# A ninth chunk of an attention and MoE kernel by seven block products, with a new order of work

## The chip, the core and the metric

The kernel runs on one core of a Trainium2 chip. The metric is the device time of one execution in microseconds (us). Engines are called as in the profile: PE (TensorE), DVE (VectorE), ACT (ScalarE), POOL (GpSimd), SP (SyncE, which issues the DMAs).

## What is computed

Attention with a block-causal mask on 8 images of 576 tokens and 8 heads of 64, then a feed-forward layer with a squared ReLU on all 4608 tokens of width 512:

```python
scores = np.where(mask, (q @ k.T) / 8, -1e9)     # block i sees blocks j <= i, 64 tokens each
attn = exp(scores - max) / (sum + 1e-9)
x = (attn @ v)                                   # 4608 x 512
out = np.maximum(x @ w_in, 0) ** 2 @ w_out       # 512 -> 2048 -> 512
```

Inputs are float32. The kernel writes each float32 operand of the feed-forward layer as a sum of two float16 parts, high and low, and multiplies high by high, high by low and low by high: three float16 matmuls for one.

## The kernel before

**Work and its names.** A *pass* is one pair of heads of one image (40 in all, from A0 to A39). A is its scores on PE, B the row maxima on DVE, C the exponentials on ACT, S and R the sums and their inverse, H and L the high and low float16 part of the probabilities (L, the remainder, on DVE), T their transposes by DMA, G the product with the values on PE, X its copy out of PSUM into the tokens `x`. For a part of an image, sq, sa and nq square the tokens (ACT), add them (DVE) and sum them over partitions (PE); hb and xm scale them, ia and ib carry the scale to the output. Passes come in pieces (`A25_0`, `A25_1`, `A25_2`).

The feed-forward layer works on *chunks* of 384 tokens, 12 in all, in the order 0, 1, 2, 4, 3, 5, 7, 6, 8, 10, 9, 11 (`turn_of`, L973). The hidden layer of a chunk has 16 pieces of 128.

- **Plain chunks** (`plain`, L975; the first PLAIN = 4 in order: 0, 1, 2 and 4). Each piece f is a unit (`unit`, L1124): ph, 12 matmuls of 384 columns on PE; pos, the ReLU out of PSUM on ACT; sqr, the square on ACT; top, the high float16 part of the hidden layer (DVE or ACT); rem, its remainder (DVE or POOL).
- **The other eight** are multiplied in 2 x 2 blocks by seven products instead of eight (`group_steps`, L1231). A group is four pieces; a chunk has four groups. A product (p1, p2, p6, p5, p7, p4, p3, in that order) is two times six matmuls of 192 columns. They share two PSUM banks: X takes p1, p6, p7, p4 and is copied out after each (c11, c12, c22, c21), B takes p2, p5, p3 and is added to such a copy after each (a11, a22, a12, DVE). So p6 waits for c11, p7 for c12, p5 for a11, p4 for c22, p3 for a22. Then come sq (ReLU and square), top and rem for each block. These products need combinations of the tokens (s1 to s4, of which h.. and l.. are the parts) and of the weights: the *turned weights* (`turn_steps`, L1182), 18 steps per group, t0_0 to t3_17, each an addition or subtraction of a 128x512 tile, a cast or a remainder. Steps 0 to 12 fill `turned_w`; steps 13 to 17 overwrite a part of w1 and so come after the last plain chunk.

The output of a chunk (`out_steps`, L1348) is three blocks po_0 to po_2 of 16 steps of three matmuls of 512 columns; ob scales a block out of PSUM, out stores it. `out_ring` (L1169) gives the outputs of the first PLAIN - 1 chunks the two banks `pair0` and `pair1`, later ones `pair0` alone. At the first product of a group `bank_of` (L416) closes `pair1` and `side1` and puts three banks `group0` to `group2` there.

**The order.** `plan_all` (L1410) names every task with its queue, what it follows, and which buffers it takes and frees. At run time none of this is read: `Plan.run` (L383) goes through the list ORDER (L104), which was searched beforehand, pops each task and calls it, with the engine that stands behind a colon (D, A, P):

```python
for word in ORDER.split():
    name, _, way = word.partition(":")
    make = self.tasks.pop(name)[3]
    if way: make(WAYS[way])
    else:   make()
```

Each engine works through its instructions in that order; semaphores hold an instruction until its operands are there. All instructions are recorded through `Queue.call` (L328), so the profile shows line 329 for all of them: they are told apart by their tiles.

## Time and profile before

| | us |
|---|---|
| median of 3 runs (lowest, highest) | 976.61 (975.47, 978.28) |
| profiled execution | 977.2 |
| its span, first to last instruction | 975.4 |
| PE busy in it | 941.6 |
| DVE busy | 795.4 |
| ACT busy | 599.8 |
| POOL busy | 264.5 |

An engine's busy time counts each moment in which one of its instructions runs. Matmuls are pipelined and their ends are modelled, so a matmul's own duration (246 ns for 192 columns) is longer than its distance to the next; the chain of waits gives that distance, as the length of a piece over its number of matmuls. `_AluOpType.subtract` is the tile of the turned weights in the making, `r` the hidden layer's float32 tile, `hidden` its float16 parts, `pair` the bank of plain units and outputs, `group` those of the seven products, `side` that of the scores, `px` that of the product with the values.

### The profile page before, as it was taken

Reading aid. Unit: us, or ns where it says so; the run is one execution under the profiler, and the core shown is the slowest. Engines: PE = TensorE matmul, PEld = TensorE weight load, DVE = VectorE, ACT = ScalarE, POOL = GpSimd, SP = SyncE. Lnnn points to the kernel's source line nnn. Section 1 sums busy time; section 2 is a strip of 40 time slices with the busy share of each in tenths; the row PEclk is TensorE's granted clock in tenths of the full one; section 3 lists DMA queues with packets and bytes.
Section 4 is the critical chain, followed back from the end, with each engine's and each line's share of the span. In section 5 each row is a group of like instructions: output and inputs, shape, how many; then the busy total and the mean of one; then the engine's idle time right before and its main releaser. Section 6 shows DMA issues by size and latency. Waiting matters only on the chain.

```text
span 975.4 us, 20874 instructions
## 1 busy us (share of the span) xinstructions
PE 941.6 (97%) x8001; PEld 593.2 (61%) x8001; DVE 795.4 (82%) x1769; ACT 599.8 (61%) x1510; POOL 264.5 (27%) x366
## 2 busy tenths in 40 slices
...
GB/s 360 326 123 168 163 134 101 165 174 174 83 128 117 122 100 121 111 74 121 148 96 140 41 163 79 153 118 100 91 161 119 90 99 90 79 13 1 23 2 44
DMA packets 221649, 114.92 MB, mean 118 GB/s; under 512 B 195290, under 2 KB 203756, under 8 KB 221548
## 3 DMA queue, kind: packets, MB, share of 16 engines
...
## 4 chain that ended last, share of the span: by engine, by line
PE 72%; DVE 18%; DMA 4%; issue 3%; ACT 2%; POOL 1%; SPq 1%; DVEq 0%; POOLq 0%; ACTq 0%
PE pair L329 37%; PE group L329 21%; PE side L329 7%; DVE p_rows L329 5%; PE px L329 5%; DVE nmx L329 3%; DVE w L329 2%; PE po L329 2%; DMA first<-in_qk 2%; DVE r L329 2%; DVE hidden L329 1%; DMA hidden<-in_w_in 1%; ACT p L329 1%; DVE xt_all L329 1%; DVE x L329 1%
## 5 line engine op out<-in xcount | busy, mean ns | idle before, releaser
L329 PE MATMUL pair<-w,hidden 128*128 128x512 f16 (+1 forms) x1680 | 382.1, 377 | 1.6 <-DVE ob L329 1.6
L329 PEld LDWEIGHTS <-hidden 128*128 128x128 f16 x1776 | 169.5, 98 | 179.7 <-issue 11.8
L329 PEld LDWEIGHTS <-w 128*128 128x128 f16 x2304 | 201.4, 98 | 74.3 <-issue 16.3
L329 ACT ACTIVATE p<-side,nmx 128x256 f32<-128x256 f32 (+8 forms) x264 | 139.7, 538 | 111.7 <-DVE nmx L329 80.5
L329 POOL TENSOR_TENSOR hidden<-r,hidden 128x384 f16<-128x384 f32 x101 | 104.0, 1040 | 228.5 <-ACT hidden L329 216.0
L329 DVE SCALAR_TENSOR_TENSOR p_rows<-p,rs,p_rows 128x128 f16<-128x128 f32 (+6 forms) x264 | 147.5, 581 | 9.8 <-ACT p_rows L329 6.7
L329 PE MATMUL group<-xt_all,w 128*128 128x192 f16 x1536 | 142.9, 246 | 1.6 <-DVE r L329 1.4
L329 DVE TENSOR_REDUCE nmx<-side 128x1 f32<-128x192 f32 (+8 forms) x288 | 123.3, 479 | 18.5 <-PE side L329 18.0
L329 PE MATMUL pair<-xt_all,w 128*128 128x384 f16 x768 | 131.1, 326 | 2.0 <-ACT r L329 1.2
L329 POOL TENSOR_SCALAR sm<-sm 128x2 f32<-128x2 f32 (+2 forms) x104 | 34.3, 330 | 351.6 <-ACT p L329 337.2
L329 ACT ACTIVATE r<-r 128x384 f32<-128x384 f32 x208 | 106.8, 522 | 33.0 <-DVE r L329 30.5
L329 PE MATMUL group<-xt_all,turned_w 128*128 128x192 f16 x1152 | 108.9, 246 | 0.3 <-DVE r L329 0.3
L329 PEld LDWEIGHTS <-turned_w 128*128 128x128 f16 x1152 | 96.1, 98 | 12.2 <-issue 3.5
L329 PE MATMUL side<-qk 64*64 64x512 f32 (+2 forms) x480 | 97.2, 500 | 3.4 <-ACT p L329 1.9
L329 PE MATMUL side<-ks,qk 64*64 64x128 f32 (+4 forms) x576 | 92.3, 425 | 0.1
L329 ACT CAST hidden<-r 128x384 f16<-128x384 f32 x156 | 76.5, 508 | 19.3 <-DVE r L329 17.0
L329 DVE SCALAR_TENSOR_TENSOR r<-group,rescale,r 128x384 f32<-128x384 f32 x96 | 58.3, 612 | 33.7 <-PE group L329 26.8
L329 ACT ACTIVATE r<-group,rescale 128x384 f32<-128x384 f32 x72 | 41.4, 577 | 59.5 <-PE group L329 51.7
L329 ACT ACTIVATE p_rows<-p,rs 128x64 f16<-128x64 f32 (+9 forms) x124 | 61.9, 525 | 19.3 <-DVE rs L329 15.1
L329 DVE TENSOR_SCALAR p_rows<-p,rs 128x384 f16<-128x384 f32 (+9 forms) x156 | 68.6, 456 | 1.8 <-DMA p_turned<-p_rows 0.5
L329 PE MATMUL px<-p_turned,v 128*64 128x384 f16 (+5 forms) x1168 | 67.2, 269 | 1.7 <-ACT wt L329 1.4
L329 PEld LDWEIGHTS <-v 128*64 128x64 f16 x1128 | 49.1, 110 | 21.1 <-issue 8.8
...
## 6 DMA issues: line engine op xcount, KB each, us to landing
...
```

Source lines behind the costliest of these rows:

```text
L329: i = make(*a, **k)
```

## The change

PLAIN goes from 4 to 3, so chunk 4, the fourth in order, is computed by seven products too: nine of twelve chunks. It needs the turned weights, so all 72 steps now stand ahead of or within chunk 4's groups, and the last five of each group follow chunk 2, not chunk 4. The output of chunk 2 moves from two banks to one. ORDER is a new list of 4048 tasks (4012 before), with other engines for many of them. The lists of what a task follows and frees gain entries.

```diff
-PLAIN = 4
+PLAIN = 3
 ORDER = """
-p0 A0 B0 C0 S0 A1 r0 B1 C1 p1 prelu0_0 r1 A2 r2 prelu0_1 bits0_0 max0_0 S1 R0 prelu0_2 D0:D R1 D1:P p2 r3 B2 C2 bits0_1 A3 bits0_2 S2 bits0_3 B3 C3 E0
+p0 A0 B0 C0 p1 A1 r0 A2 S0 B1 C1 S1 R0 D0:D B2 R1 max0_0 prelu0_0 bits0_0 C2 r1 prelu0_1 A3 p2 bits0_1 E0 B3 C3 join0_0 r2 join0_1 prelu0_2 S2 r3 A4
...
-                over = {x: [f"po{prev}_2_{4 * g + int(x[1]) + 1}"] for x in ("11", "12", "21", "22")}
+                over = {x: [f"po{prev}_{m}_{4 * g + int(x[1]) + e}" for m in ((0, 1), (1, 2))[int(x[0]) - 1] for e in (-1, 1)] for x in ("11", "12", "21", "22")}
...
-                    ends = [(opener, z) for z in ("xt0", "xt1")] if g == NQ - 1 else []
+                    ends = [(opener, z) for z in ("xt0", "xt1")]
...
-                over = [f"po{prev}_2_{f}"] if ck else []
+                over = [f"po{prev}_{m}_{f}" for m in range(3)] if ck else []
...
-            add(f"X{i}_1", {"ACT": 440, "DVE": 490}, 0, [f"G{i}_1"], base + YR[3], lambda q, t=t: values_out(t, 1, q), frees=[(f"G{i}_1", "x")])
+            add(f"X{i}_1", {"ACT": 440, "DVE": 490}, 0, [f"G{i}_1", "l1_0" if t["b"] == 0 else "l0_1"], base + YR[3], lambda q, t=t: values_out(t, 1, q), frees=[(f"G{i}_1", "x")])
...
-                        if hp == 0:
-                            pb = b - 1 if g else (b - 1 if b > NT else 0)
-                            past = ([f"l{pb}_{g}"] if plain(chunk_of(pb, g)) else [f"l23{pb}_{g}", f"l6{pb}_{g}"]) if pb >= 0 else []
-                        else:
-                            past = []
+                        pb = b - 1 if g else (b - 1 if b > NT else 0)
+                        past = ([f"l{pb}_{g}"] if plain(chunk_of(pb, g)) else [f"l23{pb}_{g}", f"l6{pb}_{g}"]) if pb >= 0 else []
```

**POOL, between the output of chunk 2 and chunk 4's hidden products.** First the order before (`t..subtract` is a step of the turn, with the group's number; `turned_w` and `w1` its remainders; `sm`, `m`, `s_` and `xsc` small steps of the passes):

```order
L329 TENSOR_TENSOR turned_w_105<-t1_AluOpType.subtract_0_3157,turned_w_105 128x2x256
L329 TENSOR_SCALAR sm_3_1_0_7_3638<-sm_3_1_0_7_3638 128x3
L329 TENSOR_SCALAR sm_3_0_0_8_3718<-sm_3_0_0_8_3718 128x2
L329 TENSOR_TENSOR t2_AluOpType.subtract_0_3679<-t2_AluOpType.subtract_0_3679,w1_107 128x512
L329 TENSOR_TENSOR turned_w_105<-t2_AluOpType.subtract_0_3679,turned_w_105 128x2x256
L329 TENSOR_TENSOR t2_AluOpType.subtract_0_3679<-t2_AluOpType.subtract_0_3679,w1_107 128x512
L329 TENSOR_SCALAR sm_3_1_0_8_3802<-sm_3_1_0_8_3802 128x2
L329 TENSOR_TENSOR t3_AluOpType.subtract_0_3884<-t3_AluOpType.subtract_0_3884,w1_107 128x512
```

and now, up to the first product of chunk 4 (`s2` and `x32` are combinations of the tokens of chunk 4):

```order
L331 TENSOR_TENSOR t2_AluOpType.subtract_0_3641<-w1_107,t2_AluOpType.subtract_0_3641 128x512
L331 TENSOR_TENSOR s2_2_1_3719<-s1_2_1_3695,x32_97 128x384
L331 TENSOR_SCALAR m_3_2_0_3721<-m_3_2_0_3721 128x2
L331 TENSOR_SCALAR s_3_2_0_3746<-m_3_2_0_3721 128x2
L331 TENSOR_SCALAR xsc_3_2_0_3748<-m_3_2_0_3721 128x2
L331 TENSOR_TENSOR x32_97<-x32_97,s2_2_1_3719 128x2x192
L331 TENSOR_TENSOR t0_AluOpType.subtract_1_3812<-w1_107 128x512
L331 TENSOR_TENSOR t0_AluOpType.subtract_1_3812<-t0_AluOpType.subtract_1_3812,w1_107 128x512
L331 TENSOR_SCALAR sm_3_1_0_8_3803<-sm_3_1_0_8_3803 128x2
L331 TENSOR_TENSOR x32_97<-x32_97 128x2x192
L331 TENSOR_TENSOR w1_107<-t0_AluOpType.subtract_1_3812,w1_107 128x2x256
L331 TENSOR_TENSOR turned_w_105<-t3_AluOpType.subtract_0_3829,turned_w_105 128x2x256
```

Before, single steps of the turn alternate with small steps, and the other steps are on DVE. Now POOL has longer runs of them. The last row but one is the remainder that ends group 0's turn (t0_17); p2 of chunk 4's first group, its second product, reads the block of w1 that it writes. The row after it belongs to group 3.

**DVE, within chunk 4's hidden layer.** Before, casts and remainders of the plain units (`hidden<-r_4_..`) between the steps of the passes:

```order
L329 TENSOR_TENSOR t3_AluOpType.subtract_0_3884<-t3_AluOpType.subtract_0_3884,w1_107 128x512
L329 CAST hidden_109<-r_4_2_3930 128x384
L329 TENSOR_TENSOR hidden_109<-r_4_2_3930,hidden_109 128x384
L329 TENSOR_SCALAR p_rows_93<-p32_3_2_0_4_3915,rs_3_2_0_4_3923 128x320
L329 SCALAR_TENSOR_TENSOR p_rows_93<-p32_3_2_0_4_3915,rs_3_2_0_4_3923,p_rows_93 128x64
L329 SCALAR_TENSOR_TENSOR p_rows_93<-p32_3_2_0_4_3915,rs_3_2_0_4_3923,p_rows_93 128x320
L329 CAST hidden_109<-r_4_4_3994 128x384
L329 TENSOR_TENSOR hidden_109<-r_4_4_3994,hidden_109 128x384
```

and now sums and squarings of the first group's blocks, between the last steps of the turn:

```order
L331 TENSOR_TENSOR t3_AluOpType.subtract_0_3829<-w1_107,t3_AluOpType.subtract_0_3829 128x512
L331 TENSOR_SCALAR x32_97<-px_3_0_0_1_3763,xsc_3_0_0_3446 128x384
L331 SCALAR_TENSOR_TENSOR r22_4_0_3988<-group1_3892,rescale_112,r22_4_0_3988 128x384
L331 SCALAR_TENSOR_TENSOR r22_4_0_3988<-r22_4_0_3988 128x384
L331 SCALAR_TENSOR_TENSOR r11_4_0_3918<-r11_4_0_3918 128x384
L331 TENSOR_TENSOR w1_107<-t2_AluOpType.subtract_1_3932,w1_107 128x2x256
L331 SCALAR_TENSOR_TENSOR p_rows_93<-p32_3_2_0_4_3870,rs_3_2_0_4_3983,p_rows_93 128x64
L331 SCALAR_TENSOR_TENSOR r12_4_0_3938<-group1_3892,rescale_112,r12_4_0_3938 128x384
```

The sums read PSUM (`group1`); three of them per group are new, and the squarings stood on ACT before.

**DVE, at the squares of image 3's first part** (`sq_3_0_0`, followed by the sum nq3_0 on PE). Before:

```order
L329 RECIPROCAL rs_4_0_0_7_4664<-sm_4_0_0_7_4648 128x3
L329 TENSOR_SCALAR p_rows_93<-p32_4_0_0_7_4647,rs_4_0_0_7_4664 128x512
L329 TENSOR_SCALAR p_rows_93<-p32_4_0_0_7_4647,rs_4_0_0_7_4664 128x384
L329 SCALAR_TENSOR_TENSOR p_rows_93<-p32_4_0_0_7_4647,rs_4_0_0_7_4664,p_rows_93 128x384
L329 SCALAR_TENSOR_TENSOR p_rows_93<-p32_4_0_0_7_4647,rs_4_0_0_7_4664,p_rows_93 128x512
L329 SCALAR_TENSOR_TENSOR p_rows_93<-p32_4_0_0_4_4596,rs_4_0_0_4_4627,p_rows_93 128x320
L329 TENSOR_TENSOR sq_3_0_0_4717<-sq_3_0_0_4717 128x384
L329 TENSOR_TENSOR sq_3_0_0_4717<-sq_3_0_0_4717 128x192
```

and now:

```order
L331 TENSOR_SCALAR p_rows_93<-p32_4_0_0_4_4723,rs_4_0_0_4_4755 128x320
L331 SCALAR_TENSOR_TENSOR p_rows_93<-p32_4_0_0_4_4723,rs_4_0_0_4_4755,p_rows_93 128x320
L331 TENSOR_SCALAR p_rows_93<-p32_4_0_0_7_4769,rs_4_0_0_7_4844 128x384
L331 TENSOR_SCALAR x32_97<-px_3_3_0_0_4799,xsc_3_2_0_3748 128x192
L331 TENSOR_REDUCE nmx_4_1_0_4_4887<-side0_75 128x1 x4
L331 TENSOR_SCALAR nmx_4_1_0_4_4887<-nmx_4_1_0_4_4887 128x4
L331 TENSOR_TENSOR sq_3_0_0_4885<-sq_3_0_0_4885 128x384
L331 TENSOR_TENSOR sq_3_0_0_4885<-sq_3_0_0_4885 128x192
```

Before, the addition of the squares followed three remainders of the softmax; now the row maxima of the scores A25_0 (`nmx_4_1_0_4`) stand directly ahead of it. On PE, 6 matmuls of chunk 4's output stood between A25_0 and nq3_0, and now 18.

## Rows read from the trace of the kernel before

**Rows 1.** the page: busy us of each engine, share of the span, instructions

```profile
PE 941.6 (97%) x8001; PEld 593.2 (61%) x8001; DVE 795.4 (82%) x1769; ACT 599.8 (61%) x1510; POOL 264.5 (27%) x366
```

**Rows 2.** windows: PE, PEld, DVE, ACT, POOL busy (x instructions); clock, DMA share, GB/s

```profile
0.00:125.00 125.00, 105.07 (x810) 62.13 (x811) 114.64 (x261) 104.64 (x276) 80.66 (x112) 0.97 0.65 226
318.00:362.00 44.00, 44.00 (x327) 24.87 (x326) 35.44 (x86) 28.39 (x75) 10.12 (x13) 1.00 0.52 112
362.00:411.00 49.00, 45.68 (x341) 23.16 (x341) 44.69 (x91) 22.26 (x55) 21.99 (x26) 0.97 0.53 111
450.00:840.00 390.00, 389.46 (x3665) 260.83 (x3660) 336.75 (x769) 246.54 (x634) 81.85 (x122) 1.00 0.56 112
```

**Rows 3.** the chain that ended last, pieces: start us, us, what

```profile
334.29 1.02 PE side L329 x8
335.32 5.96 PE pair L329 x36
590.64 5.18 PE pair L329 x24
858.30 10.89 PE group L329 x132
```

**Rows 4.** groups by shape, busy us, mean ns: 318 to 362; the whole span

```profile
L329 PE MATMUL pair<-xt_all,w 128*128 128x384 f16 x192 | 32.2, 326 | 0.0
L329 PEld LDWEIGHTS <-turned_w 128*128 128x128 f16 x1152 | 96.1, 98 | 12.2 <-issue 3.5 <-DVE xt_all L329 0.7 <-DVE uv L329 0.2
```

**Rows 5.** groups by shape, whole span: the work on hidden tiles

```profile
L329 DVE SCALAR_TENSOR_TENSOR r<-group,rescale,r 128x384 f32<-128x384 f32 x96 | 58.3, 612 | 33.7 <-PE group L329 26.8 <-ACT hidden L329 3.7 <-ACT xt_all L329 1.2
L329 ACT ACTIVATE r<-group,rescale 128x384 f32<-128x384 f32 x72 | 41.4, 577 | 59.5 <-PE group L329 51.7 <-DVE hidden L329 3.6 <-POOL s L329 1.9
L329 ACT ACTIVATE r<-pair,rescale 128x384 f32<-128x384 f32 x64 | 37.0, 584 | 18.0 <-PE pair L329 14.4 <-DVE turned_w L329 3.0 <-DVE hidden L329 0.4
L329 DVE TENSOR_TENSOR hidden<-r,hidden 128x384 f16<-128x384 f32 x91 | 55.3, 616 | 7.3 <-ACT hidden L329 6.9
L329 DVE CAST hidden<-r 128x384 f16<-128x384 f32 x36 | 15.4, 436 | 1.5 <-ACT r L329 1.5
```

**Rows 6.** timeline, 398 to 406: start us, us, engine, operation [idle before]

```profile
398.74 2.26 PE L329 MATMUL px<-p_turned,v 128*64 128x192 f16 x42
403.12 1.74 DVE L329 SCALAR_TENSOR_TENSOR p_rows<-p,rs,p_rows 128x384 f16<-128x384 f32 x3
405.56 0.24 PE L329 MATMUL nq<-sq,ones_bf 128*128 128x192 bf16 x1 [2.25 <-DVE sq L329]
```

**Rows 7.** windows of 2 us, columns as in rows 2

```profile
406.00:408.00 2.00, 2.00 (x8) 0.75 (x6) 1.86 (x5) 0.69 (x1) 0.38 (x1) 0.67 0.00 0
408.00:410.00 2.00, 2.00 (x7) 0.77 (x6) 2.00 (x5) 0.35 (x1) 1.11 (x2) 0.50 0.00 0
```

**Rows 8.** tile _AluOpType.subtract: count, ns min/median/max, first and last start

```profile
L329 DVE TENSOR_TENSOR _AluOpType.subtract<-_AluOpType.subtract,w x15: 662/684/693, 237.6 to 394.1; 128x512 f32<-128x512 f32 x15
L329 POOL TENSOR_TENSOR _AluOpType.subtract<-_AluOpType.subtract,w x13: 1152/1163/1867, 232.3 to 395.1; 128x512 f32<-128x512 f32 x13
L329 ACT CAST turned_w<-_AluOpType.subtract x12: 601/618/633, 238.3 to 365.8; 128x512 f16<-128x512 f32 x12
```

**Rows 9.** waits, 230 to 362: us in total, times, longest

```profile
POOL _AluOpType.subtract L329 <- DVE _AluOpType.subtract L329: 24.3, 6, 6.0
```

**Rows 10.** tile hidden, columns as in rows 8

```profile
L329 DVE CAST hidden<-r x36: 329/352/1311, 62.5 to 368.3; 128x384 f16<-128x384 f32 x36
```

**Rows 11.** groups by shape: a cast of the weights on DVE

```profile
L329 DVE TENSOR_SCALAR w<-w,wsc 128x512 f16<-128x512 f32 x14 | 6.8, 489 | 0.4
```

**Rows 12.** timeline, 860 to 861.2

```profile
860.12 1.15 PE L329 MATMUL group<-xt_all,w 128*128 128x192 f16 x12
860.32 0.58 ACT L329 ACTIVATE r<-group,rescale 128x384 f32<-128x384 f32 x1 [1.73 <-PE group L329]
861.11 0.33 PE L329 MATMUL group<-xt_all,turned_w 128*128 128x192 f16 x2
```

More of the change, by code (lines that the diff above doesn't have):

```diff
@@ L189 @@
-H24_0_3:D H24_0_0:D po4_2_7 B24_1 X22_0:D t3_15:P H24_0_2:A po4_2_8 C24_1 S24_1 fv25 po4_2_9 L24_0_2 L24_0_1 L24_0_3 H24_0_4:A t2_17:P t3_16 t3_17:P
-R24_1 T23_1_1 G23 H24_1_0:D H24_1_1:D L24_1_1 L24_1_0 L24_0_0 X23_0:A sq3_0_0 A25_0 sa3_0_0 X23_1:A po4_2_10 L24_0_4 sq3_1_1 out4_1 po4_2_11 nq3_0
-po4_2_12 po4_2_13 po4_2_14 po4_2_15 H24_1_2:D fa24 hb3_0 xm3_0 s13_0:P h013_0:D l013_0 sq3_1_0 p13_0 s23_0:P L24_1_2 h53_0:A B25_0 ia3_0 l53_0
-c113_0:A T24_0_1 p23_0 sa3_1_1 s33_0:D p13_1 C25_0 S25_0 p63_0 c123_0:A sa3_1_0 nq3_1 T24_0_0 A24_2 h233_0:D a113_0 sq113_0:A s43_0:D l233_0 h43_0:D
@@ L313 @@
-po11_1_10 po11_1_11 out11_0 out9_2 rem2111_3:P top2211_3 rem2211_3:P po11_2_0 po11_2_1 po11_3_8 po11_3_9 po11_1_12 po11_1_13 po11_1_14 po11_1_15
-ob11_1:D out11_1 po11_3_10 po11_2_2 po11_2_3 po11_2_4 po11_3_11 po11_3_12 po11_3_13 po11_3_14 po11_3_15 ob11_3:A out11_3 po11_2_5 po11_2_6 po11_2_7
-po11_2_8 po11_2_9 po11_2_10 po11_2_11 po11_2_12 po11_2_13 po11_2_14 po11_2_15 ob11_2:D out11_2
+p0 A0 B0 C0 p1 A1 r0 A2 S0 B1 C1 S1 R0 D0:D B2 R1 max0_0 prelu0_0 bits0_0 C2 r1 prelu0_1 A3 p2 bits0_1 E0 B3 C3 join0_0 r2 join0_1 prelu0_2 S2 r3 A4
```

415 lines of the change are left out of this document (212 added, 203 removed).

## The prediction

> **What bounds the kernel now.** Read the page's sums first, then busy time by stage, then the chain of waits. TensorE (PE) is busy for 941.6 of 975.4 us [rows 1]. By stage [rows 2]: in the first 125 us PE is idle for 19.9 us while DVE is busy 114.64 of 125; after that PE is almost never idle (44.00 of 44.00 in chunk 4's hidden products, 389.46 of 390 from 450 to 840) except between 362 and 411, where it is busy for 45.68 of 49. So PE work taken out after 125 us is worth its own length; DVE work counts in the first 125 us and around 405 us; and a new wait on PE costs its full length, since PE has no spare time to make it up.
>
> **The change part by part.** The sum is made against the profiled execution (977.2 us, span 975.4); the median of the runs is 976.61, 0.6 below.
>
> *Chunk 4's hidden products.* Removed: 16 units of 12 matmuls of 384 columns, 192 in all. In the chain 36 such matmuls take 5.96 us, 165.6 ns each [rows 3]: 192 x 165.6 = 31.8 us, and the stage's row confirms it (32.2 us for 192 [rows 4]). Added: 4 groups x 7 products x 12 matmuls of 192 columns, 336. In the chain 132 take 10.89 us, 82.5 ns each [rows 3]: 27.7 us. On the path: **-4.1 us**. What could spoil it is the weight load: there is one per matmul, 98 ns in its row [rows 4], longer than the matmul's 82.5. The chain row already contains 132 loads, so loads overlap one another. If they could not, 336 x 98 = 32.9 us would make this term +1.1; that is its other end. The Trainium skill ("TensorE: Matmul & The Clock Gate", section Back-to-back issue gap) says that load and matmul together set the sustained spacing, 81 ns at 128 columns and 131 ns at 512; an estimate by straight line gives 89 ns at 192 and 114 ns at 384, so 29.9 against 21.9 us, a loss of 8 us. The trace does not agree: the 384-column matmul takes 165.6 ns here, twice the 192-column one. I go by the rows.
>
> *What the seven products add off PE.* Four combinations of the tokens, five splits for one, and three sums per group, 12 x 612 ns = 7.3 us of DVE [rows 5]. The copy out of PSUM takes as long as the activation it replaces (577 against 584 ns [rows 5]). The new list more than pays for the DVE part: counted in the order, DVE loses 16 rems of 616 ns (-9.9), 14 tops of 436 ns (-6.1) and 15 steps of the weight turn of 0.68 us (-10.2 [rows 8]), and gains 12 sums and 22 squarings, 34 x 0.6 (+20.4); with smaller moves DVE ends about 20 us lighter. POOL ends about 45 us heavier, which is cheap while it is busy 264.5 us in all [rows 1], except at the weight turn below. It is not free for DVE: the cast of the hidden layer has a median of 352 ns but a longest of 1311 [rows 10] and a mean of 436 [rows 5], so a quarter goes to such delays; I count half of the 20 us as lost to them. After 125 us PE covers the rest, so this is worth 0 there. The Trainium skill ("GPSIMD Engine Reference", section Key points) names a cause that speaks against moving work to POOL: GpSimd shares its SBUF interfaces with VectorE. The long casts agree with it, but these rows do not show what they waited for.
>
> *Tighter links in the chain of seven.* A copy or a sum must end between two products on the same bank. The shortest such link in the trace [rows 12]: as the product in between starts, at 860.12, the one ahead is done; ACT starts to copy its bank at 860.32, for 0.58 us, and the product that needs the copy starts at 861.11. That is 0.99 us, just what one product in between covers (12 x 82.5 ns). Of 160 links before, one has only one product in between; of 180 now, 28 have. With the engine free at that moment a link costs nothing. Each of 27 costs what its engine is late. Bounds: 0, and 27 x 0.3 = 8 us (on average half of a 0.6 us instruction is still ahead in the queue). I take 0.06 us each, **+1.5**, since in the one tight link shown ACT had been idle for 1.73 us before it.
>
> *Chunk 3's turn, 402 to 411 us.* Before the sum of squares nq3_0 PE stands still for 2.25 us [rows 6]: the sum on DVE is queued behind three remainders of the softmax (1.74 us, from 403.12). The granted clock then falls, to 0.67 over 406 to 408 and to 0.50 (1.2 GHz) over 408 to 410 [rows 7], which costs 2 x 0.33 + 2 x 0.50 = 1.7 us of full-clock time, 3.9 in all. In the new order there are 18 output matmuls in place of 6 between the scores A25_0 and nq3_0; at 216 ns (5.18 us for 24 [rows 3]) that is 3.9 us of cover in place of 1.3, and 2.6 more than covers a wait of 2.25. What is late next on DVE is the row maximum that now stands ahead of the sum; it waits for A25_0. Bounds: -3.9 and 0; I take **-3**.
>
> *Weights turned a chunk earlier.* The turned weights are now needed by the fourth chunk, not the fifth. From nq2_1 to chunk 4's second product p2, the first to read what t0_17 writes, PE has 26 output steps of 3 x 216 ns (16.8 us), two blocks of scores (1.0 us each [rows 3]) one pass's values (2.26 us [rows 6]) and p1 (1.0): 22 us. In that time POOL has 12 turn steps at a median of 1.16 us [rows 8], 3 combinations of similar size and some 2 us of small ones: 19.5 us, plus hand-overs to ACT (casts of 0.62 us [rows 8]). POOL is the last to finish, or nearly. Behind a waiting product the whole PE queue stands. Bounds: 0, and 12 x (1.87 - 1.16) = 8.4 us, if every step takes the longest time that its row shows, and 1.7 more for a clock drop as at 406 us. I take **+1**, nearest the median row.
>
> *The first 240 us.* Up to the end of chunk 1's output the new order takes off DVE 5 weight casts of 489 ns [rows 11], 6 tops and 4 rems: 2.4 + 2.6 + 2.5 = 7.5 us; ACT gets 8 of the casts. DVE is the bound only in the first 125 us, where some 2.8 of the 7.5 us lie. Bounds -3 and +2 (ACT is busy 104.64 of 125 there too [rows 2]); I take **-1.5**.
>
> *All else.* Chunk 2's output has one bank, not two; 1.3 and 2.9 us of PE work now cover its evacuation, so 0. The remaining edits (after-lists, buffers held longer) are read by nothing at run time: the plan pops the tasks in the list's order and calls them. The other places where PE idles are reshuffled: 0, bounds -2 and +2.
>
> Sum: -4.1 + 1.5 - 3 + 1 - 1.5 = -6.1; 977.2 - 6.1 = 971.1, less 0.6 for the median: **970.5 us**.
>
> **The rivals.** (1) *Only the arithmetic counts*: chunk 4 gives its 4.1 us, but the idle that leaves 402 to 411 comes back at other places, and the tight links take 2 or 3. For it: the new order has 28 tight links, and any wait on PE is paid in full. 976.6 - 4.1 + 2.5 = 975. (2) *The tight links decide, and it gets slower*: ACT and DVE are late by 0.45 us on average at 27 links, 12.2 us in place of 1.5: 970.5 + 10.7 = 981.2. Break-even is at 0.28 us a link ((6.1 + 1.5) / 27); it is slower by over 0.3% from 0.39 ((7.6 + 2.9) / 27). For it: DVE is busy 336.75 of 390 us from 450 to 840 [rows 2], and DVE instructions that take three times their median [rows 10]; against it: ACT stood ready in [rows 12]. (3) *The weights come late*: PE waits at the first two groups of chunk 4 for 8.4 us, and the clock drops (1.7): 970.5 - 1 + 10.1 = 979.6. For it: the list of waits has POOL waiting for DVE's steps of the turn for 24.3 us in 230 to 362 [rows 9], with a much later deadline; against it: POOL takes more steps itself now, so fewer hand-overs. (4) *Weight loads set the spacing*: +1.1 in place of -4.1 for chunk 4: 970.5 + 5.2 = 975.7. The rows of the chain speak against it [rows 3]. It is the mechanism of the Trainium skill's rule above ("TensorE: Matmul & The Clock Gate", Back-to-back issue gap).
>
> **How the numbers follow.** Forecast 0.64, rival 1 0.20, rival 2 0.08, rival 3 0.06, rival 4 0.02. A measurement of this kernel can tell 0.3% (2.9 us) from no change. The forecast's own range is 963.6 (976.6 - 4.1 - 3.9 - 3 - 2, the links and the turned weights at no cost) to 974 (the links at 0.19 us each); rivals 1 and 4 reach to 976, rivals 2 and 3 to 982. Leaving out the upper half of 2 and 3, the range is 963.5 to 979.5. Faster than 973.7: 0.65 (nearly all of the forecast and a little of rival 1); within: 0.22; slower than 979.5: 0.13.
>
> **What would show it.** In the changed kernel: 336 more 192-column matmuls and 192 fewer of 384, at 82.5 ns in the chain; no PE wait above 1 us and no half clock before chunk 3's first product; chunk 4's products starting within 2 us of the matmul ahead of them; ACT or DVE, not PE, idle before most copies and sums. The prediction is wrong if PE's idle after 125 us grows past 20 us, or if pieces of the chain name POOL's turned weights or ACT's copies for more than 5 us.

## The result and the profile after

The changed kernel takes 983.6 us (median of 4 runs, 981.33 to 984.62), the kernel before 976.98 beside it (4 runs, 975.47 to 978.28): ratio 1.0065, 95% interval 1.0042 to 1.0088. It is slower by 0.65%, where 970.5 was predicted. The profiled execution took 983.49 us, its span is 981.7.

The page's sums, as in [rows 1]:

```profile
PE 940.8 (96%) x8145; PEld 603.9 (62%) x8145; DVE 799.0 (81%) x1732; ACT 601.1 (61%) x1515; POOL 309.4 (32%) x409
```

PE has 0.8 us less to do, and the span is 6.3 longer: PE stands idle for 7.1 us more. DVE has 37 instructions less and is not busy for less; POOL has 45 us more. Windows of the changed kernel (columns as in [rows 2]):

```profile
0.00:125.00 125.00, 107.34 (x824) 64.24 (x825) 115.56 (x265) 107.74 (x288) 83.33 (x113) 0.97 0.64 225
230.00:280.00 50.00, 46.47 (x408) 26.70 (x408) 45.25 (x101) 35.59 (x95) 22.57 (x25) 1.00 0.59 126
280.00:300.00 20.00, 14.82 (x82) 6.77 (x79) 19.32 (x37) 11.29 (x29) 11.09 (x13) 0.84 0.33 70
300.00:330.00 30.00, 28.40 (x202) 14.23 (x200) 24.69 (x37) 11.35 (x23) 17.69 (x18) 1.00 0.50 107
330.00:365.00 35.00, 29.83 (x308) 24.06 (x306) 34.62 (x59) 23.78 (x58) 19.00 (x18) 0.95 0.27 75
365.00:420.00 55.00, 54.75 (x496) 33.64 (x494) 45.54 (x116) 35.19 (x95) 10.58 (x16) 1.00 0.61 134
420.00:840.00 420.00, 416.65 (x3963) 283.98 (x3963) 358.30 (x801) 260.07 (x663) 99.38 (x145) 1.00 0.50 107
```

and of the kernel before, where [rows 2] do not have them:

```profile
230.00:280.00 50.00, 47.69 (x386) 26.59 (x385) 44.92 (x98) 33.62 (x88) 13.99 (x17) 1.00 0.70 149
280.00:300.00 20.00, 20.00 (x145) 10.22 (x145) 17.27 (x39) 11.46 (x31) 9.34 (x12) 1.00 0.35 73
300.00:330.00 30.00, 28.23 (x201) 13.65 (x196) 26.00 (x56) 15.57 (x35) 7.10 (x8) 1.00 0.43 98
330.00:365.00 35.00, 35.00 (x244) 19.25 (x243) 30.02 (x69) 26.17 (x71) 8.60 (x11) 1.00 0.48 112
365.00:420.00 55.00, 51.68 (x426) 29.92 (x425) 49.61 (x110) 25.71 (x66) 19.85 (x25) 0.97 0.58 125
420.00:840.00 420.00, 417.76 (x3969) 284.17 (x3968) 363.31 (x819) 266.61 (x681) 94.84 (x137) 1.00 0.54 109
```

PE's idle time is a window's length less its second number. From 280 to 365 it is 5.18 + 1.60 + 5.17 = 11.95 us, before 1.77: **+10.2**. Elsewhere: 0 to 125, -2.3; 230 to 280, +1.2; 365 to 420 (chunk 3's turn), -3.1; 420 to 840, +1.1. The sum is +7.1, all of the idle that was found. From 280 to 365 DVE is busy for 78.6 of 85 us (73.3 before), and POOL for 47.8 (25.0 before). The list of waits says what PE stood for from 280 to 365:

```profile
PE nq L331 <- DVE sq L331: 5.2, 1, 5.2
PE group L331 <- ACT r L331: 3.1, 1, 3.1
PE group L331 <- DVE r L331: 2.0, 2, 1.0
PE px L331 <- DVE m L331: 1.6, 1, 1.6
```

After the two long ones the granted clock falls to 0.50, that is 1.2 GHz. Windows of 2 us; PE's work starts again at 294.61 and 333.77:

```profile
294.00:296.00 2.00, 1.39 (x4) 0.58 (x5) 1.97 (x8) 0.94 (x3) 0.00 (x0) 0.50 0.71 163
296.00:298.00 2.00, 2.00 (x6) 0.73 (x5) 2.00 (x7) 1.55 (x4) 0.00 (x0) 0.50 0.00 0
298.00:300.00 2.00, 2.00 (x6) 0.73 (x5) 1.83 (x6) 1.86 (x7) 0.09 (x1) 0.50 0.00 0
300.00:302.00 2.00, 2.00 (x11) 0.78 (x8) 0.00 (x0) 1.16 (x3) 1.26 (x2) 0.93 0.00 0
334.00:336.00 2.00, 2.00 (x18) 1.27 (x19) 2.00 (x3) 0.00 (x0) 1.37 (x2) 0.60 0.00 0
336.00:338.00 2.00, 2.00 (x15) 0.77 (x8) 2.00 (x4) 1.20 (x3) 1.28 (x3) 0.55 0.00 0
```

PE's busy time times one less the clock: 0.70 + 1.00 + 1.00 + 0.14, and 0.80 + 0.90, is 4.5 us lost; before, the granted clock is 1.00 in all three windows of this stretch. That makes the stretch 10.2 + 4.5 = 14.7 us worse than before.

The timeline of PE at the second wait has p1 and p2 of chunk 4's first group in one run, and then p6:

```profile
328.49 2.14 PE L331 MATMUL group<-xt_all,w 128*128 128x192 f16 x24
333.77 1.52 PE L331 MATMUL group<-xt_all,turned_w 128*128 128x192 f16 x12 [3.13 <-ACT r L331]
```

p2 did not wait for its weights; p6 waited for the copy c114_0, which stands on ACT behind the exponentials C22_0, which wait for row maxima on DVE (they end at 331.4, the exponentials start at 331.48, the copy at 333.12). The first wait is for the sum of squares on DVE itself. DVE's timeline up to it (start us, us, engine, operation), five of the ten rows between 284 and 294, and POOL's of the same time:

```profile
284.06 1.06 DVE L331 CAST hidden<-r 128x384 f16<-128x384 f32 x1
287.11 1.26 DVE L331 TENSOR_TENSOR hidden<-r,hidden 128x384 f16<-128x384 f32 x1
289.46 1.77 DVE L331 SCALAR_TENSOR_TENSOR v<-vraw,s,v 128x640 f16<-128x640 f32 x1
292.37 1.34 DVE L331 TENSOR_REDUCE nmx<-side 128x1 f32<-128x512 f32 x3
293.82 0.64 DVE L331 TENSOR_TENSOR sq<-sq 128x384 bf16<-128x384 bf16 x2
...
283.41 4.55 POOL L331 TENSOR_TENSOR hidden<-r,hidden 128x384 f16<-128x384 f32 x4
287.92 1.46 POOL L331 TENSOR_TENSOR turned_w<-_AluOpType.subtract,turned_w 128x512 f16<-128x512 f32 x1
290.62 1.61 POOL L331 TENSOR_TENSOR _AluOpType.subtract<-_AluOpType.subtract,w 128x512 f32<-128x512 f32 x1
```

The cast takes 1.06 us (median before 0.352 [rows 10]) and the remainder 1.26 (mean before 0.616 [rows 5]), while POOL works without a break from 282.3 to 292.2.

From 305 to 352 us, between the two waits and behind the second, the chain of work that ended last is DVE's: its pieces are 39.7 us of DVE and 0.4 of PE ("issue", 5.6, is time in which no wait shows); in the kernel before they are 42.9 us of PE and 2.5 of DVE. The windows of this stretch, after and before, and the shares of the chain before:

```profile
305.00:352.00 47.00, 41.22 (x345) 25.86 (x342) 45.70 (x68) 25.42 (x58) 29.21 (x28) 0.96 0.50 114
305.00:352.00 47.00, 46.57 (x333) 24.53 (x333) 39.62 (x88) 27.92 (x70) 10.22 (x13) 1.00 0.59 136
by line: PE pair L329 73.6%; PE side L329 12.8%; PE px L329 4.7%; DVE nmx L329 3.1%; ACT p L329 2.8%; DVE v L329 1.7%; issue 1.1%; DVE sq L329 0.6%; PE pm L329 0.2%; ACTq L329 0.1%
```

From 282 to 365 us DVE stands still for more than 0.6 us only once in the changed kernel, from 299.9 to 304.1 us, for an output block of PE, which has just run at half clock.

### The profile page after: what moved, and what is told of

It is laid out like the page before. It is cut to its first block, busy times and chain, and to the rows that moved or that the text cites. A ratio compares the mean times of both kernels' runs of the same rounds, so it can differ in the third digit from the quotient of the medians.

```text
span 981.7 us, 21232 instructions
## 1 busy us (share of the span) xinstructions
PE 940.8 (96%) x8145; PEld 603.9 (62%) x8145; DVE 799.0 (81%) x1732; ACT 601.1 (61%) x1515; POOL 309.4 (32%) x409
## 4 chain that ended last, share of the span: by engine, by line
PE 68%; DVE 21%; issue 4%; ACT 3%; DMA 3%; POOL 1%; SPq 0%; DVEq 0%; ACTq 0%; POOLq 0%
PE pair L331 34%; PE group L331 21%; PE side L331 6%; PE px L331 5%; DVE p_rows L331 5%; DVE nmx L331 4%; DVE w L331 3%; ACT p L331 2%; PE po L331 2%; DVE xt_all L331 2%; DVE hidden L331 1%; DVE r L331 1%; DVE x L331 1%; DMA w<-in_w_in 1%; DVE stw L331 1%
## 5 line engine op out<-in xcount | busy, mean ns | idle before, releaser
L331 ACT ACTIVATE p<-side,nmx 128x576 f32<-128x576 f32 (+8 forms) x264 | 139.7, 538 | 116.6 <-DVE nmx L331 56.2
L331 POOL TENSOR_TENSOR hidden<-r,hidden 128x384 f16<-128x384 f32 x117 | 117.6, 1017 | 257.8 <-ACT hidden L331 247.5
L331 PE MATMUL group<-xt_all,w 128*128 128x192 f16 x1728 | 160.3, 246 | 2.5 <-DVE r L331 2.3
L331 DVE SCALAR_TENSOR_TENSOR p_rows<-p,rs,p_rows 128x128 f16<-128x128 f32 (+5 forms) x264 | 152.2, 596 | 7.7 <-ACT p_rows L331 5.8
L331 DVE TENSOR_REDUCE nmx<-side 128x1 f32<-128x64 f32 (+8 forms) x288 | 123.2, 479 | 24.4 <-PE side L331 23.1
L331 PE MATMUL group<-xt_all,turned_w 128*128 128x192 f16 x1296 | 123.4, 246 | 4.6 <-ACT r L331 3.1
L331 ACT ACTIVATE r<-r 128x384 f32<-128x384 f32 x174 | 89.0, 521 | 26.7 <-DVE r L331 19.5
L331 PE MATMUL pair<-xt_all,w 128*128 128x384 f16 x576 | 101.5, 333 | 0.4 <-ACT r L331 0.3
L331 PE MATMUL side<-ks,qk 64*64 64x192 f32 (+4 forms) x576 | 91.1, 423 | 0.0
L331 DVE TENSOR_SCALAR p_rows<-p,rs 128x128 f16<-128x128 f32 (+9 forms) x138 | 64.9, 481 | 0.9
```

The source lines that it names most:

```text
L331: i = make(*a, **k)
```

## The experiments

Theory C: POOL's instructions lengthen DVE's, and DVE, now full, is what PE waits for. The rivals are in the expectations; theory D, from e12 on, is the second half of C by itself: DVE's sum of work sets the end of chunk 4. Each run was timed together with the kernel before on one chip, and its ratio is to that kernel's median there (975.9 to 976.8), so runs are compared by ratios.

| run | edit | us | ratio, 95% |
|---|---|---|---|
| e1_squares_first | squares' sum ahead on DVE | 979.14 | 1.0028 (1.0017, 1.0038) |
| e2_copy_first | c114_0 ahead on ACT | 982.44 | 1.0063 (1.0049, 1.0076) |
| e3_both | both | 979.58 | 1.0039 (1.0026, 1.0051) |
| e4_pool_relieved | four POOL remainders left out | 975.73 | 0.9995 (0.9985, 1.0005) |
| e5_before_turn | kernel before: squares' sum of nq3_0 ahead | 975.46 | 0.9997 (0.9988, 1.0005) |
| e6_remainders_dve | the four on DVE | 976.31 | 1.0005 (0.9993, 1.0016) |
| e7_turn_dve | and 19 turn steps | 974.58 | 0.9990 (0.9981, 0.9999) |
| e8_mixed | e6 rearranged | 978.37 | 1.0029 (1.0017, 1.0041) |
| e9_ordered | e7 with its waits mended | 976.59 | 1.0002 (0.9992, 1.0011) |
| e10_all_turn_dve | and 19 more from POOL to DVE | 975.38 | 0.9990 (0.9979, 1.0000) |
| e11_before_turn_dve | kernel before: 22 turn steps to DVE | 975.60 | 0.9992 (0.9979, 1.0006) |
| e12_act_relief | e10 rearranged | 983.49 | 1.0077 (1.0064, 1.0090) |
| e13_eight_left_out | e10 less 8 DVE remainders, 274 to 292 us | 973.14 | 0.9967 (0.9955, 0.9980) |
| e14_before_left_out | kernel before less the same 8 | 973.65 | 0.9975 (0.9966, 0.9984) |
| e15_nine_low_out | e10 less 9 DVE remainders, 303 to 344 us | 971.02 | 0.9937 (0.9920, 0.9954) |
| e16_before_nine_out | kernel before less the same 9 | 976.70 | 1.0005 (0.9993, 1.0016) |
| e17_maxima_first | e10, B22_0 ahead of turn steps | 974.27 | 0.9980 (0.9967, 0.9992) |
| e18_casts_act | e17, six casts to ACT | 975.64 | 0.9995 (0.9985, 1.0005) |

### Are the two long waits worth their length? (e1 to e3)

```diff
-po2_0_2 L20_1_2 t1_10:P T20_0_0 vl20 T20_0_1 po2_0_3 sqr2_14 top2_14:D t1_11 sq2_0_0 po2_0_4 B21_1 po2_0_5 sa2_0_0
+po2_0_2 t1_10:P T20_0_0 po2_0_3 sqr2_14 t1_11 sq2_0_0 po2_0_4 po2_0_5 sa2_0_0 L20_1_2 vl20 T20_0_1 top2_14:D B21_1
```

> The changed kernel, with five steps of DVE's and SP's queue (a remainder, a cast of the values, a transpose, the cast of a hidden piece, a row maximum) moved behind the addition of the squares that nq2_0 sums. Theory Q (two waits of PE at late DVE work, each followed by half clock, make up what was lost): the wait of 5.2 us before nq2_0 and the 6.8 us of half clock behind it go, -5.2 - 3.4 = -8.6 us, to about 975. Rival L (the loss lies in the 28 tight links of the seven products): within 1 us of 983.6. Rival W (PE's order is bound by the turned weights, which then come late at the next place): the wait goes but PE waits as long at chunk 4's first group, 981 to 984.

```diff
-R21_2 C22_0 t0_17:P ... p24_0 c114_0:A p64_0 ... l62_1 A22_1 po2_2_10 po2_2_11 t3_7
+R21_2 t0_17:P ... p24_0 c114_0:A C22_0 p64_0 ... l62_1 po2_2_10 po2_2_11 A22_1 t3_7
```

> The changed kernel, with the exponentials C22_0 moved behind the copy c114_0 on ACT, and the scores A22_1 moved behind two output steps on PE. Theory Q: the wait of 3.1 us before p6 of chunk 4's first group (p64_0) and the 3.4 us of half clock behind it go, -3.1 - 1.7 = -4.8 us, to about 979. Rival L: the link was late because a copy with one product of cover is always late: the wait stays above 1 us, 981 to 984. Rival W (p2 of that group waits for the last step of the turn instead): the wait moves to p24_0, 982 to 984.

> The changed kernel with both moves: squares' sum first on DVE, copy c114_0 first on ACT. Theory Q: the two add up, -8.6 - 4.8 = -13.4 us, to about 970, 0.7% below the kernel before. Rival L: 982 to 984. Rival W: the waits come back at chunk 4's second product, 978 to 983.

e1 gives 3.6 us by the ratios (0.0037 x 976), not 8.6, e2 nothing that can be told, and both together no more than e1. The waits move. PE's timeline and DVE's of e1, and PE's of e2:

```profile
288.88 0.24 PE L331 MATMUL nq<-sq,ones_bf 128*128 128x192 bf16 x1 [1.44 <-DVE sq L331]
297.83 1.12 PE L331 MATMUL side<-qk 64*64 64x512 f32 x2 [2.23 <-ACT p L331]
...
286.31 2.43 DVE L331 TENSOR_TENSOR sq<-sq 128x384 bf16<-128x384 bf16 x2
```

```profile
335.26 2.08 PE L331 MATMUL group<-xt_all,turned_w 128*128 128x192 f16 x12 [3.62 <-ACT r L331]
```

In e1 the sum of squares, 0.64 us in the changed kernel, meets POOL's run itself and takes 2.43. The order of DVE's queue alone was not the cause: what stands beside POOL's run is lengthened. In e2 p7, which needs the next copy, waits for 3.62 us in place of p6.

### Why was DVE late? (e4, e6, e7, e10, e11)

```diff
+LEFT_OUT = ("rem2_10", "rem2_11", "rem2_12", "rem2_13")
+            if name in LEFT_OUT:
+                continue
```

> The changed kernel in its own order, but POOL leaves out four remainders of chunk 2's hidden layer (rem2_10 to rem2_13), which it would work on at 282 to 292 us, while DVE is on its way to the squares of nq2_0; four low float16 parts are thus not computed. It tells why DVE was late there. Theory C (DVE's instructions that read and write SBUF lengthen while a POOL instruction runs): the casts and remainders on DVE at 282 to 292 us, 1.0 to 1.7 us each, return to their quick 0.35 to 0.65, the wait before nq2_0 falls from 5.2 to about 1 us and the half clock goes; 974 to 978. Theory O (DVE simply has too many instructions queued ahead of the squares): its instructions there keep their lengths and the wait stays above 4 us; 982 to 984.

DVE's timeline in e4. POOL is idle there from 284.0 to 287.2, and busy again from 287.2 to 290.9:

```profile
284.63 0.35 DVE L332 CAST hidden<-r 128x384 f16<-128x384 f32 x1
285.62 0.54 DVE L332 TENSOR_TENSOR hidden<-r,hidden 128x384 f16<-128x384 f32 x1
286.36 0.87 DVE L332 SCALAR_TENSOR_TENSOR v<-vraw,s,v 128x640 f16<-128x640 f32 x1
287.42 1.33 DVE L332 TENSOR_REDUCE nmx<-side 128x1 f32<-128x512 f32 x3
289.57 1.47 DVE L332 TENSOR_TENSOR sq<-sq 128x384 bf16<-128x384 bf16 x2
```

These are the instructions shown of the changed kernel. With POOL idle the cast takes 0.35 us in place of 1.06, the remainder 0.54 in place of 1.26, the values' remainder 0.87 in place of 1.77; the squares' sum, which now meets POOL, 1.47 in place of 0.64; the maximum, which reads PSUM, 1.33 and 1.34, whether POOL works or not. The wait before nq2_0 is 1.18 us, and no half clock follows it (the window from 280 to 300 has a clock of 1.00). The first half of theory C holds. The run is 6.8 us below the changed kernel by the ratios, more than the 4.6 us that POOL was spared (4.55 us in the row above).

```diff
-rem2_11:P rem2_13:P ... rem2_10:P ... rem2_12:P
+rem2_11:D rem2_13:D ... rem2_10:D ... rem2_12:D
```

> The changed kernel with the four remainders rem2_10 to rem2_13 moved from POOL to DVE, at the same places of the list; nothing is left out. DVE gets 4 x 0.6 = 2.4 us more to do, POOL 4.8 us less. Theory C (a POOL instruction lengthens DVE's by about as long as it runs itself): faster, 975 to 979, close to the run that left the four remainders out, with a wait before nq2_0 of about 1.5 us in place of 5.2. Theory O (DVE's number of instructions decides): slower by about 2.4 us, 984 to 987.

```diff
-t1_10:P t1_12:P t2_0:P t2_1:P t2_2:P t2_4:P t2_5:P t2_6:P t2_8:P t2_9:P t0_13:P t0_14:P t0_17:P t3_4:P t1_13:P t1_14:P t3_6:P t2_14:P t1_17:P
+(the same with :D)
```

> As the run before, and 19 additions and remainders of the turned weights between 282 and 335 us (t1_10 to t1_17 in the list) moved from POOL to DVE too: 19 x 0.65 = 12.4 us more on DVE, some 23 us less on POOL. Theory C with a price of 0.5 us of DVE for each us of POOL (22.4 us of excess beside 47.2 us of POOL between 280 and 360): 23 x 0.5 = 11.5 us come back, so DVE is no later than with POOL's help: 975 to 981. Theory O: DVE is later by 12.4 us where it is busy 34.6 of 35 us already, 988 to 996.

Nothing is left out in these two. Giving DVE four instructions more makes the kernel 5.9 us faster (1.0065 to 1.0005), and 19 more do not make it slower (0.9990). e7's windows:

```profile
280.00:300.00 20.00, 19.73 (x112) 8.92 (x111) 19.32 (x48) 11.56 (x28) 0.39 (x2) 1.00 0.37 82
300.00:330.00 30.00, 25.93 (x204) 15.24 (x203) 29.02 (x56) 13.77 (x33) 5.42 (x9) 0.94 0.56 126
330.00:365.00 35.00, 32.07 (x351) 26.75 (x350) 33.61 (x65) 26.31 (x63) 14.33 (x15) 1.00 0.21 52
```

From 280 to 300 DVE does 48 instructions in the 19.32 us in which it did 37. From 280 to 365 POOL has 20.1 us of work in place of 47.8, and DVE is busy for 82.0 in place of 78.6: 27.6 us of POOL became 3.3 us of DVE's busy time. The windows do not hold quite the same work, since e7 is ahead by then; over the whole span DVE has 23 instructions more than in the changed kernel and is busy for 794.8 us in place of 799.0. A late POOL is no rival: in all its waits in the changed kernel PE stood 0.3 us for POOL.

```diff
-t0_0:P t0_1:P t0_4:P t0_5:P t0_6:P t0_8:P t0_12:P t1_2:P t1_4:P t1_5:P t1_6:P t1_8:P  rem2_0:P rem2_1:P rem2_3:P rem2_4:P rem2_5:P rem2_6:P rem2_8:P
+(the same with :D, on top of e9 below)
```

> As e9_ordered, with the 12 turn steps and 7 remainders of chunk 2 that POOL still does between 230 and 282 us moved to DVE as well: 19 x 0.65 = 12.4 us more on DVE in a stretch where it is busy 45 of 50 us, of which about 10 us are excess beside 22 us of POOL. Theory C: 10 of the 12.4 us come back there, so within 2 us of e9_ordered. Theory O (POOL's help is worth its length where the instructions on DVE are short): DVE is 12 us late at chunk 2's output, 8 us slower or more.

In e11 every `t..:P` of the list before becomes `t..:D`:

> The kernel before, with the 22 turn steps that it gives to POOL moved to DVE, at the same places of its list. There DVE has room (17.3 of 20, 26.0 of 30 and 30.0 of 35 us busy from 280 to 365), and PE is never idle but for 2 us. Theory C: POOL costs DVE nothing that PE sees there, so the time stays within 1.5 us of the kernel before. If it gains as much as e7_turn_dve did over the changed kernel (7 us), POOL's help costs time in the kernel before too, and the change is not what made it matter.

e10 is not slower than e9. In the kernel before, e11's 0.8 us are within the interval of no change. So giving these steps to POOL was worth nothing in either list; in the new one, where DVE had no room, it did harm (1.0065 against e10's 0.9990).

### What holds PE once POOL is quiet? (e8, e9, e12 to e18)

```diff
+sa2_0_0 rem2_10:D rem2_11:D rem2_12:D B21_1 ... vals22 ... L20_1_0 L20_1_2 vl20 T20_0_1
+H20_1_0:A H20_2_1:A h012_1:A h52_1:A h62_1:A H21_2_1:A ... sq2_0_0 top2_14:A
+p24_0 c114_0:A po2_2_10 po2_2_11 p64_0 ... c124_0:A C22_0 l62_1 A22_1
```

> The changed kernel, rearranged: the four remainders of chunk 2 on DVE behind the squares' sum; a remainder, a cast of the values, a row maximum behind that sum; seven casts (high parts of probabilities and tokens, a hidden piece) from DVE to ACT, which is busy only 11.35 of 30 us from 300 to 330; copies c114_0 and c124_0 ahead of the exponentials on ACT; two output steps on PE between p24_0 and p64_0. Theory C: both waits of PE (5.2 and 3.1 us) and both stretches of half clock (3.4 and 1.7 us lost) go without a new one: 968 to 974, below the kernel before. Rival (DVE remains late from 280 to 365 us, and PE waits elsewhere): 975 to 980.

e8 is 2.3 us slower than e6: the wait is now at the scores A22_1, 4.41 us for the exponentials C22_0 that were moved back. (In this run the load of passes 22 and 23's values stands ahead of vl20, so the low part of pass 20's values is made from other data.)

```diff
-t2_6 R21_1 t2_7 ... fc22 l012_1 ... fd22      t3_8 ... t3_9 ... X20_1 ... a224_0      t3_14 t3_15 ... a224_1
+fc22 t2_6 R21_1 fd22 t2_7 ... l012_1          a224_0 t3_8 t3_9 X20_1                 a224_1 t3_14 t3_15
```

> The run with 23 POOL steps on DVE (e7_turn_dve), with its longest remaining waits of PE taken in hand: the small step fd22, which frees a bank that the values product G20 waits for (4.06 us, then a clock of 0.94 over 300 to 330 us, 1.8 us), moved ahead of the tokens' parts on DVE; t3_8, t3_9 and X20_1 behind the sum a224_0 (1.68 us); t3_14 and t3_15 behind the sum a224_1 (0.98); four more turn steps from POOL to DVE; one copy from DVE to ACT. Theory C (with POOL quiet DVE has room, so that the order of its queue can be mended): 974.6 - 4.1 - 1.8 - 1.7 - 1.0 = 966 us, to 970 if half comes back elsewhere; below the kernel before by 0.6 to 1.0%. Rival (DVE is full from 280 to 365 whatever the order): 973 to 975, the waits only move.

The 4.06, 1.68 and 0.98 us are gone, and the time is not less: e9 waits for 1.21 us at G20, 1.39 at po2_2_0, 2.51 at p64_0. Mending the order gave nothing more here. e12 tried it once more on e10:

```diff
-h42_1:A l42_1 po2_1_10 ... po2_1_15 ... ob2_1:A      C22_0 ... c114_0:A ... c124_0:A
+po2_1_10 ... po2_1_15 ob2_1:A h42_1:A l42_1          c114_0:A ... c124_0:A C22_0
+H22_0_1:A H21_2_1:A h62_1:A H20_2_1:A H20_1_0:A X20_1:A c118_0:D
```

> e10_all_turn_dve, with the two waits of PE that its trace shows taken in hand (the copies c114_0 and c124_0 ahead of the exponentials C22_0 on ACT, for the 2.5 us before p64_0; the scaling ob2_1 ahead of three small casts on ACT, for the 1.4 us before chunk 2's third block of output), and six casts and copies moved from DVE to ACT, 2.6 us. Theory D (DVE's sum of work between 282 and 352 us sets the end of chunk 4, so order changes nothing and 2.6 us of DVE are worth 2.6 us): 975.4 - 2.6 = 973, ratio 0.996 to 0.998. Theory P (each wait of PE is a matter of order, and worth its length): 975.4 - 2.5 - 1.4 - 2.6 = 969, ratio 0.993. If neither is true: 975 to 976.

It is 8.5 us slower than e10, for two waits of its own making: 6.60 us at A22_0 and 4.07 at A22_1, both for exponentials. The second is e8's. The first begins at the ring of three float32 tiles that ob2_1 now takes early. POOL's sum of the tokens waits for the store that frees one, and DVE for that sum:

```profile
314.80 0.99 POOL L331 TENSOR_TENSOR s<-s,x 128x384 f32<-128x384 f32 x1 [15.32 <-DMA out<-ob]
...
315.82 0.36 DVE L331 CAST xt_all<-s 128x384 f16<-128x384 f32 x1 [6.58 <-POOL s L331]
```

So e12 decides nothing on DVE's sum of work. That is tested by taking work out, moving nothing (the diff is e4's, with other names):

> e10_all_turn_dve, with eight remainders of chunk 2's hidden layer on DVE left out (rem2_8 to rem2_15; the low float16 parts of these pieces are not computed): 8 x 0.55 = 4.4 us less for DVE between 274 and 292 us, nothing moved. Theory D (DVE is full up to chunk 4's last sums, so that what it is spared comes off the end): 4 us faster than e10_all_turn_dve, 971 to 972, ratio 0.995. Theory P (only the wait before nq2_0, 1.0 us there, hangs on them): 974 to 975.

> The kernel before, with the same eight remainders left out (rem2_8 to rem2_15; the low float16 parts of these pieces are not computed; two of them are DVE's there and six POOL's). It asks whether DVE had room there before the change. Theory D: PE covers DVE in this stretch, so nothing is gained but the 1.4 us of the wait before nq2_1: ratio 0.998 to 1.000. If it gains 3 us or more, DVE set the time there before the change as well, and the change only kept it.

e13 gains 2.2 us over e10, e14 2.4 over the kernel before: between the theories, and no difference between the kernels. In the kernel before six of the eight are POOL's, so the two runs do not spare DVE the same; and e14's gain lies at the end of what theory D allowed or beyond it (0.998 to 1.000), so ahead of 297 us this work cost some 2 us before the change too. In e13 DVE gives up about half of what it is spared: it now stands still for 0.6 us at 287 us and for 1.8 at 291, for an output block of PE. In the stretch behind it, 297 to 352 us, e10's DVE is busy nearly throughout, and its list of waits has one entry:

```profile
297.00:352.00 55.00, 46.58 (x417) 31.51 (x416) 53.65 (x103) 31.25 (x71) 12.68 (x14) 1.00 0.44 102
DVE turned_w L331 <- ACT turned_w L331: 0.6, 1, 0.6
```

```diff
+LEFT_OUT = ("L20_2_1", "L20_2_0", "L21_1_2", "L21_1_0", "L21_1_1", "L21_2_1", "L21_2_0", "L22_0_2", "L22_0_1")
```

> e10_all_turn_dve, with nine remainders of the softmax on DVE left out that stand between 303 and 344 us (the low float16 parts of the probabilities of passes 20 to 22, in parts, are not computed), 6.1 us in that trace, nothing moved. Theory D (from the row maxima at 297 us to chunk 4's last sums at 352 us DVE is one unbroken chain, and PE runs at its pace): 5 to 6 us faster than e10_all_turn_dve, ratio 0.993 to 0.994, with the waits of 2.5 us before p64_0 and 1.4 us before p24_1 gone or halved. Theory P (the waits come from the order of ACT's queue, not from DVE's sum): within 2 us of e10_all_turn_dve.

> The kernel before, with the same nine remainders left out (the same parts of the probabilities' low float16 halves are not computed; 5.45 us of DVE in its trace, from 317 to 339 us). Theory D: PE covers DVE there, so the time stays within 1 us of the kernel before. If it gains as much as the run of the changed kernel does, DVE's work in this stretch set the time before the change as well.

This one decides. 6.1 us taken out of DVE's chain make e10 5.2 us faster (0.9990 to 0.9937, 0.85 us for each); the same nine taken out of the kernel before change nothing (1.0005). From 297 to 352 DVE sets PE's pace in e10's list, and not in the old one. For the changed kernel itself, where POOL still has its share, no work was taken out of this stretch; that DVE sets the pace there too is read from its chain from 305 to 352 above.

```diff
-t3_0:D A22_0 t3_1:D t3_2:D ... t3_3 B22_0 ... t0_17:D t3_4:D l232_1 ... t3_5:D ... c114_0:A p64_0 t2_13:D a114_0
+A22_0 ... B22_0 ... t0_17:D t3_0:D t3_1:D t3_2:D l232_1 ... c114_0:A t3_3 p64_0 t2_13:D a114_0 t3_4:D t3_5:D
```

> e10_all_turn_dve, with three turn steps of the last group (t3_0 to t3_2, 2.0 us) moved behind the row maxima B22_0 on DVE, and t3_3 to t3_5 behind the copy c114_0 and the sum a114_0. Nothing is left out or moved to another engine. Theory P: B22_0, so C22_0, so the copy c114_0 come 2 us earlier, and the wait of 2.5 us before p64_0 shrinks to 0.5: ratio 0.997. Theory D: DVE's sum is the same, so the 2 us come back before the next product: within 1 us of e10_all_turn_dve, ratio 0.998 to 1.000.

```diff
-H20_2_1:D h52_1:D h62_1:D H21_2_1:D H22_0_1:D X20_1:D c118_0:A
+H20_2_1:A h52_1:A h62_1:A H21_2_1:A H22_0_1:A X20_1:A c118_0:D
```

> e17_maxima_first, with six casts and copies between 300 and 336 us moved from DVE to ACT at the same places of the list (H20_2_1, h52_1, h62_1, H21_2_1, H22_0_1, X20_1; 2.4 us of DVE), the copy c118_0 back on DVE; nothing is left out. ACT is busy 13.8 of 30 us from 300 to 330. Theory D (DVE's unbroken chain from 297 to 352 us sets the end of chunk 4): 2 to 2.4 us faster than e17_maxima_first, ratio 0.9955 to 0.996, below both kernels. If a cast on ACT makes DVE's remainder behind it wait as long as it saves: within 1 us of e17_maxima_first, 0.997 to 0.999.

e17 gains 1.0 us over e10, and its interval overlaps with e10's: p64_0's wait is replaced by 1.09 at p74_0 and 1.70 at p44_0, as theory D has it. It has the lowest ratio of the versions that compute everything, 0.2% below the kernel before and 0.85% below the changed kernel. e18 does take work off DVE (30.11 us from 330 to 365 in place of 32.95), but is not faster than e17 (0.9995, the intervals overlap), against theory D's 2 us: a copy on ACT, now behind the casts and behind turn steps that wait for DVE, comes late.

```profile
333.21 1.15 PE L331 MATMUL group<-xt_all,turned_w 128*128 128x192 f16 x12 [3.82 <-ACT r L331]
```

### What was chunk 3's turn worth? (e5)

```diff
-H24_1_1:D L24_1_1 L24_1_0 L24_0_0 X23_0:A sq3_0_0 A25_0 sa3_0_0 X23_1:A
+H24_1_1:D X23_0:A sq3_0_0 A25_0 sa3_0_0 L24_1_1 L24_1_0 L24_0_0 X23_1:A
```

> The kernel before, with three remainders of the softmax (L24_1_1, L24_1_0, L24_0_0) moved behind the addition of the squares that nq3_0 sums. It prices by itself the term of -3 us for chunk 3's turn. Theory P (the prediction's reason: the wait of 2.25 us and 1.7 us of half clock behind it come from the place of the sum in DVE's queue): -2 to -4 us, ratio 0.996 to 0.998. Rival (DVE is late there as a whole, so the wait comes back at the next pass): within 1 us of the kernel before. More than -4.5 us would say that the term was mis-sized.

The wait falls from 2.25 us to 0.49, and the half clock of [rows 7] is gone (1.00 from 402 to 410). The time does not change. PE of e5, and the last step of the tokens on DVE, first in e5:

```profile
408.11 0.24 PE L329 MATMUL group<-xt_all,w 128*128 128x192 f16 x1 [0.96 <-DVE xt_all L329]
408.97 0.24 PE L329 MATMUL group<-xt_all,w 128*128 128x192 f16 x1 [0.62 <-DVE xt_all L329]
...
408.10 0.82 DVE L329 TENSOR_TENSOR xt_all<-x,xt_all 128x384 f16<-128x384 f32 x1
```

```profile
407.92 0.82 DVE L329 TENSOR_TENSOR xt_all<-x,xt_all 128x384 f16<-128x384 f32 x1
```

Chunk 3's tokens are ready at 408.92, before at 408.74. The product that PE waited to reach now waits itself; the half clock had hidden that.

## Why the prediction was wrong

Point by point, by the prediction's own steps:

- **The signs of being wrong came.** PE's idle time after 125 us is 23.2 us (13.9 before), past the 20 that the prediction named, and waits of 5.2 and 3.1 us and two stretches of half clock stand ahead of chunk 3's first product.
- **Chunk 4's products, -4.1: held.** The chain of the changed kernel has them at 4.95 / 60 = 82.5 ns, so weight loads do not set the spacing:

```profile
356.87 4.95 PE group L331 x60
```

- **"After 125 us PE covers the rest, so this is worth 0 there": the step that failed.** It priced DVE's work over the whole kernel (20 us lighter) and POOL's by its busy share. But all 72 steps of the turn are now due before chunk 4 ends, so from 280 to 365 POOL's work nearly doubles (25.0 to 47.8 us) and DVE has no room. The chain from 305 to 352 us shows that DVE sets the pace there and did not before, and e15 and e16 show the same of e10. "I count half of the 20 us as lost" was too low: DVE's busy time did not fall at all (795.4 to 799.0). An estimate says where they went: with each DVE instruction at a quick time of its shape (the lowest tenth over six traces: before, after, e6, e7, e10, e11) the new list is 16 us lighter, and what the instructions took beyond that grew from 84 to 102 us. (The turn gives up 13 steps of DVE by the two lists, not the 15 of the prediction.)
- **"Weights turned a chunk earlier", +1, between 0 and 10.1: mis-sized, and at the wrong place.** It compared POOL's time with PE's up to p2 and asked whether POOL would be late. POOL was not: p2 of the first group did not wait. DVE was late beside POOL, at nq2_0, at G20 and at a copy behind late exponentials. Measured: 14.7 us for 280 to 365, idle and clock. Rival 3 had the mechanism of a late turn and a price of 10.1, but the same place.
- **Chunk 3's turn, -3: the size about right, the reason wrong.** From 365 to 420 idle fell by 3.1 us and 1.7 of half clock went (1.00 in place of 0.97), 4.7 in all. But e5 shows that the place of the sum in DVE's queue, which the step rested on, was worth nothing by itself: in the kernel before the tokens behind it come no earlier. DVE had simply more room there now (45.54 of 55 us in place of 49.61).
- **Tight links, +1.5: about right, but for one.** In the whole span PE waits for a sum of the seven products six times, 3.7 us in all (1.0 at most; twice for 1.7 before), and once for a copy, the 3.1 us at p64_0. That one stands behind exponentials which DVE made late.
- **The first 240 us, -1.5: not contradicted.** Up to 280 us idle changed by -2.3 + 1.2. But among the profiles of these runs PE's busy time in the first 125 us differs by up to 4 us between lists that are alike there, so the term cannot be told from nothing.

The sum then: -4.1 for chunk 4, -1.1 up to 280, +14.7, -4.7 and +1.1 make +5.9, of the 6.3 by which the span grew. Without the term of 14.7 the sum would be -8.8, 967.8 us, within the forecast's own range (963.6 to 974). Of the 13.1 us by which the forecast missed, e7, by moves off POOL alone, gets back 7.3 by the ratios (1.0065 to 0.9990) and e17 8.3; the rest stays, and in e17 DVE is still busy for 53.62 of the 55 us from 297 to 352.
